# Scores of 21 of 32 attention units from split queries and keys in three passes, with a re-planned order, in a fused attention and two-layer kernel

## The chip, the cores and the metric

One core of a Trainium2 chip runs the whole program. The metric is the device time of one execution in microseconds (us). TensorE does the matrix products (PE in the rows, with its weight loads as PEld), VectorE (DVE), ScalarE (ACT) and GpSimd (POOL) the elementwise work, and SyncE (SP) issues most transfers.

## The reference

```python
scores = scale * np.matmul(q, k.transpose(0, 1, 3, 2))        # 4 batches, 8 heads, 576 rows, 64 deep
scores = np.where(causal, -1000000000.0, scores)
a = np.exp(scores - scores.max(-1, keepdims=True))
a /= a.sum(-1, keepdims=True) + 1e-09
local = np.matmul(a, v)
q_p = phi(q)                                                  # max(x + 1, exp(min(x, 0)))
mem_out = (q_p @ M_prev) / (q_p @ z_prev + 1e-6)
attn_out = g * mem_out + (1 - g) * local                      # g: a sigmoid per head
x = attn_out as 2304 tokens x 512
x = leaky_relu(x @ w_in) @ w_out                              # layer 1, 512 -> 2048 -> 512
x = (h - tanh(h)) @ w2_out, with h = x @ w2_in                # layer 2, the same shape
```

## The kernel before

**Two phases.** In the first, attention is done in 32 units (16 of kind B, then 16 of kind A), each for one batch and a pair of heads. A B unit has the query rows 256 to 575 against all keys, an A unit rows 0 to 255 against 256 keys. Mixed into this phase runs layer 1 for three blocks of 256 tokens. In the second phase layer 1 for the other blocks and then layer 2 run in a fixed loop of products 512 columns wide. Lines L910 and L988 are the layer products of the first phase, L1163 and L1200 those of the second.

**A unit's steps on TensorE**: scores (`score`, L647 for the tiles of 128 rows, L652 for the last 64 rows), the memory product (`mem`, L567), transposes of the memory part (L745) and of the probabilities (L779, L767), and the product with v (`pv`, L801). Scores are plain float32 products 64 deep: head 0 lies on partitions 0 to 63 and head 1 on 64 to 127, so the two heads of a pair use two halves of the array. The layer products are of type float32r, each number split beforehand into a high and a low part, in three products.

**The order** is written by a planner before the kernel is built. `Schedule.op` declares each piece of work with its expected duration on each engine that could do it; `Schedule.run` lets time go by, and each free engine takes the first piece in order of priority whose inputs are due and whose buffers (`RINGS`) are free. Attention goes ahead of layer work (`MOE_PE`), so layer products fill TensorE where attention isn't ready. The engines then execute that order strictly, however long things take. `SWITCH` is what the plan adds when TensorE goes from one kind of product to another (`mode`), `UNITS` the order of the units, `LEND` the number of first units that borrow the layer's PSUM buffers, `W1_FROM`, `W1_STEP`, `CUT` the priority of weight conversion on VectorE and ScalarE (L838 to L854), `CALM` how far ahead weight loads may queue.

**Between the phases** (`opened`, `load2`, `split_hi`, `split_lo`): when the last unit's output is copied and stored, two blocks are loaded back, `x2i`, one after the other through a single buffer; each is split into its high part (ScalarE) and its low part (VectorE), and the second phase's first product reads both blocks. The results of the third layer-1 block are copied out of PSUM (`g<-dn`) and stored (`x2s<-g`, L1008).

Of the kernel before, what the change touches and what calls it, by code (L numbers as in the profile page):

```python
# [9 lines left out]
F32 = mybir.dt.float32  # L10
# [22 lines left out]
RINGS = {  # L33
# [10 lines left out]

SWITCH = {(0, 1): 88.0, (2, 1): 88.0, (0, 2): 45.0}

CALM = 6000.0

# [18 lines left out]
def DVE(n):  # L67
    return 69 + 1.04 * n
# [202 lines left out]

OFFSET = {"load": 0, "memory": 0.3, "scores": -1, "values": 0.6}

MZ_APART = True

LEND = 6

LENT = ((0, 15), (1, 15), (1, 14))

UNITS = [(k, b, hp, hp % 2 if k == "A" or b < 1 else 0) for k in "BA" for b in range(4) for hp in range(4)]  # L280

# [3 lines left out]

AHEAD = 5

BIAS = {"act": 1.0, "dve": 1.5, "pool": 1.1}

W1_FROM, W1_STEP = (7.7, 15.7), 0.002  # L290

NARROW = 3

CUT = 2


@with_exitstack
def kernel(
# [14 lines left out]
    nc = tc.nc  # L313
# [159 lines left out]
    class Unit:  # L473
# [11 lines left out]
        def rows(self, t):  # L485
            return REST if t == 4 else 128

        def declare(self, pr, prev):
            kind, b, hp = self.kind, self.b, self.hp
# [13 lines left out]

            qk, v_ = new("qk"), new("v" if kind == "B" else "va")
            n0 = 0 if kind == "A" else NA
            qc, kc = (0, NA) if kind == "A" else (S, 0)

            def load_qk(e):
                qk.tile = att.tile([128, 896], F32, name="qk", bufs=RINGS["qk"])
# [82 lines left out]
            op([("dve", DVE(nqc))], phi_max, reads=[qk, ph], writes=[ph])  # L592
            order["p"] = op([("pe", nq * 195)], mem, reads=[ph, mz], alloc=[s, mo], after=in_order("p"))
            free_op([("dve", 75)], den_gate, reads=[s, gates], alloc=[dn], port=False)
            free_op([("dve", 110)], den_inv, reads=[dn], writes=[dn], port=False)
            free_op([("dve", DVE(nf))], mem_out, reads=[s, dn], writes=[mo], port=False)

            part_ = "scores"
# [6 lines left out]

            for tiles in ([[0, 1]] if kind == "A" else [[2], [3], [4]]):
                if not self.lend:
# [18 lines left out]
                def score(e, tiles=tiles, ss=ss):  # L626
# [6 lines left out]
                    for t in tiles:  # L633
                        nn, i, en = min(S, (t + 1) * 128), t - q0, et[t - q0].tag
                        if en[0] == "h":
                            m_, f_ = LENT[t - 2]
                            et[i].tile = wts.tile([128, 640] if t == 4 else [128, 2, nn], F32, name=f"w{m_}_{f_}")
                        else:
                            et[i].tile = att.tile([128, 640] if t == 4 else [128, 2, nn], F32, name=en, bufs=RINGS[en])
                        _, mx, c0 = made[t]  # L640
                        mx.tile = att.tile([128, 2], F32, name="mx", bufs=RINGS["mx"])
                        a, half = qc + i * 128, nn // 2
                        for k in range(1 if t < 4 else 2):
                            for j in range(2):
                                p = slice(64 * j, 64 * j + 64)
                                if t < 4:
                                    nc.tensor.matmul(  # L647
                                        ss[j].tile[:, c0:c0 + nn], lhsT=qk.tile[p, a:a + 128],
                                        rhs=qk.tile[p, kc:kc + nn], start=True, stop=True)
                                    continue  # L650
                                c = (j + k) % 2
                                nc.tensor.matmul(  # L652
                                    ss[c].tile[p, 0:half], lhsT=qk.tile[p, a:a + REST],
                                    rhs=qk.tile[p, kc + c * half:kc + (c + 1) * half], start=True, stop=True)

                order["s"] = op([("pe", {384: 847, 512: 1060, 576: 1117}[width])], score, reads=[qk], mode=1,
                                alloc=ss + [h for t in tiles for h in (et[t - q0], made[t][1])],
                                after=in_order("s") if tiles[0] == q0 else [order["s"]])
            for i in range(nq):
# [88 lines left out]

            op([("pe", nq * 109 - 60)], mem_tr, mode=2, reads=[mo], alloc=[o])
            pts, parts = {}, []  # L750
            for kt in range(nk):
# [35 lines left out]
                for j in range(len(ss)):  # L787
                    fresh = j == 0 and kt < 4
                    order["e"] = op(
                        [("pe", (nq - i0) * 109 * (3 - len(ss)) - 60)], lambda e, j=j, f=tr_e: f(e, j), mode=2,  # L790
                        reads=[et[i] for i in range(i0, nq)] + ([] if fresh else [pt]),
# [250 lines left out]
    for kind, b, hp, alt in UNITS:  # L1042
        u = Unit(kind, b, hp)
        u.alt, u.lend = alt, u_at < LEND
        u.declare((0, u_at), prev)
# [276 lines left out]
```

## Time and profile before

| | |
|---|---|
| median of 3 runs | 1019.87 us (1017.53 to 1020.28) |
| the profiled execution | 1019.15 us, of which the span of its instructions is 1017.4 |
| TensorE busy | 995.1 us of the span |
| VectorE, ScalarE, GpSimd busy | 702.8, 629.6, 196.9 us |
| first product of the second phase | 359.36 us after the start |

The profile page gives busy time per engine, the granted TensorE clock in slices, the chain of work that ended last and the costliest groups of instructions. Matmul durations in it overlap, since the engine is a pipeline: the pace of a stretch is read from the distance between starts.

### The profile page before, as it was taken

To read this page: it belongs to the slowest core of one execution; us is meant where nothing else is said; L and a number is where in the kernel's file an instruction comes from. 1 tells how busy PE (TensorE), PEld (TensorE's weight loads), DVE (VectorE), ACT (ScalarE), POOL (GpSimd) and SP (SyncE) were. 2 spreads that over 40 slices of the span, in tenths; PEclk is the share of its full clock that TensorE was granted. 3 is DMA by queue.
4 is the path that set the end of the run, shared out by engine and by line. 5 is a ranking of instruction groups with operands and counts; after the bars stand their busy time and mean duration, and the time that the engine had idled before them with its cause. 6 is when DMAs were issued, how large, how long until landed. Compare 5 with 4: busy or idle time off the path is not lost.

```text
span 1017.4 us, 16055 instructions
## 1 busy us (share of the span) xinstructions
PE 995.1 (98%) x5664; PEld 817.5 (80%) x5664; DVE 702.8 (69%) x1592; ACT 629.6 (62%) x1325; POOL 196.9 (19%) x174
## 2 busy tenths in 40 slices
PE   5899999999999999999999999999999999999998
PEld 3577877778888988888888888888888888888897
DVE  7999999555577366758650225877787787777775
ACT  6987787666598244334423436866676676676664
POOL 1100000000000022222224553222222222222221
PEclk9999999999999999999999999999999999999999
DMA  9564622212252156446534333100100100010010
GB/s 273 188 184 128 192 91 70 69 49 70 59 154 79 63 161 221 144 138 196 184 106 142 117 94 94 43 1 0 63 21 1 63 22 1 1 62 1 1 43 21
DMA packets 92993, 91.77 MB, mean 90 GB/s; under 512 B 45296, under 2 KB 72944, under 8 KB 92912
## 3 DMA queue, kind: packets, MB, share of 16 engines
q1 hardware_dynamic: 91696, 89.44, 28.5%
q10 hardware_dynamic: 1216, 1.31, 0.4%
q8 instruction: 44, 0.72, 0.3%
q14 instruction: 37, 0.30, 0.1%
HBM read 69.75 MB, written 20.97 MB: 89 GB/s over the span
## 4 chain that ended last, share of the span: by engine, by line
PE 91%; DVE 5%; DMA 2%; ACT 1%; issue 1%; SPq 0%; ACTq 0%
PE up L1163 32%; PE dn L1200 32%; PE up L910 6%; PE dn L988 6%; PE o L801 4%; PE s L779 4%; PE s L647 3%; DMA qk<-in_qkt_dram 2%; PE s L567 1%; PE o L745 1%; PE s L652 1%; DVE e L673 1%; DVE cv L849 1%; DVE w L673 1%; DVE e L729 0%
## 5 line engine op out<-in xcount | busy, mean ns | idle before, releaser
L1163 PE MATMUL up<-xs,w 128*128 128x512 f32 (+1 forms) x1536 | 346.1, 375 | 0.0
L1163 PEld LDWEIGHTS up<-xs,w 128*128 128x128 f32 x1536 | 275.8, 188 | 52.9
L468 POOL TENSOR_TENSOR gl<-gf,gh 128x512 fp32r<-128x512 f32 x119 | 154.9, 1301 | 591.7 <-ACT gh L1150 579.5
L1200 PE MATMUL dn<-w,gh 128*128 128x512 f32 x576 | 174.8, 389 | 0.0
L1140 DVE SCALAR_TENSOR_TENSOR gf<-u,w 128x512 f32<-128x512 f32 x72 | 83.8, 1165 | 67.7 <-ACT w L1137 67.6
L1200 PEld LDWEIGHTS dn<-w,gh 128*128 128x128 f32 x576 | 107.6, 188 | 22.0
L1200 PE MATMUL dn<-gh,w 128*128 128x512 f32 x384 | 118.3, 389 | 0.0
L1200 PE MATMUL dn<-w,gl 128*128 128x512 f32 x288 | 109.5, 389 | 0.0
L1117 ACT ACTIVATE gf<-up 128x512 f32<-128x512 f32 x48 | 28.6, 597 | 119.7 <-PE up L1163 116.4
L1131 ACT ACTIVATE u<-up 128x512 f32<-128x512 f32 x72 | 43.0, 598 | 91.8 <-PE up L1163 91.6
L693 ACT ACTIVATE e<-e,mx 128x256 f32<-128x256 f32 (+4 forms) x134 | 76.0, 569 | 21.8 <-DVE mx L673 13.6
L910 PE MATMUL up<-xs,w 128*128 128x256 f32 x576 | 86.8, 290 | 0.0
L1150 ACT ACTIVATE gh<-gf 128x512 fp32r<-128x512 f32 x120 | 74.6, 621 | 16.9 <-DVE gf L1143 16.8
L1200 PEld LDWEIGHTS dn<-gh,w 128*128 128x128 f32 x384 | 72.1, 188 | 15.0
L910 PEld LDWEIGHTS up<-xs,w 128*128 128x128 f32 x576 | 73.6, 189 | 4.7 <-issue 4.7
L1200 PE MATMUL dn<-gl,w 128*128 128x512 f32 x192 | 74.7, 389 | 0.0
L1200 PEld LDWEIGHTS dn<-w,gl 128*128 128x128 f32 x288 | 54.0, 188 | 11.3
L455 ACT ACTIVATE pt<-s 128x320 f32<-128x320 f32 (+4 forms) x132 | 52.7, 440 | 15.9 <-PE s L779 9.3
L673 DVE CUSTOM_DVE_ANT_0 e<-s,mask 128x128 f32<-128x128 f32 (+4 forms) x114 | 46.8, 455 | 22.3 <-PE s L647 19.3
L779 PE MATMUL s<-identr,e 128*128 128x128 f32 x404 | 56.9, 279 | 4.4 <-ACT e L727 1.8
L1143 DVE COPY_PREDICATED gf<-mk,up 128x512 f32<-128x512 int32 x72 | 53.7, 746 | 7.4
L988 PE MATMUL dn<-gh,w 128*128 128x256 f32 x384 | 54.7, 286 | 0.4 <-ACT gh L455 0.4
(130 smaller groups left out, 1506.2 us busy)
## 6 DMA issues: line engine op xcount, KB each, us to landing
w<-in_moe_w_out_dram SPq DMA_DIRECT2D x16, 512.0 KB, 5.5
w<-vs SPq DMA_DIRECT2D x32, 256.0 KB, 2.6
qk<-in_qkt_dram SPq DMA_DIRECT2D x16, 448.0 KB, 3.6
w<-in_moe_w_in_dram SPq DMA_DIRECT2D x14, 512.0 KB, 5.8
v<-in_v_dram SPq DMA_DIRECT2D x16, 320.0 KB, 3.1
x2i<-x2s SPq DMA_DIRECT2D x9, 512.0 KB, 4.1
qk<-in_qkt_dram SPq DMA_DIRECT2D x16, 256.0 KB, 2.8
u<-in_moe_w_in_dram SPq DMA_DIRECT2D x16, 256.0 KB, 2.9
```

The source lines that it names most:

```text
L455: nc.scalar.activation(out=out, in_=in_, func=AF.Copy)
L468: (nc.vector if e == "dve" else nc.gpsimd).tensor_tensor(out=out, in0=in_, in1=high, op=ALU.subtract)
L673: nc.vector.tensor_tensor_reduce(out=out, in0=in0, in1=in1, scale=-scale, scalar=mx.tile[:, 0:1] if t == 4 and j else BIG, op0=ALU.add, op ...
L693: nc.scalar.activation(out=x, in_=x, func=AF.Exp, scale=-1.0, bias=mx.tile[:, k:k + 1], accum_out=sm.tile[:, 2 * i + j:2 * i + j + 1])
L779: nc.tensor.transpose(ss[j].tile[:, a:a + 128], x, ident)
L910: nc.tensor.matmul(ps()[:, s, :], lhsT=w[:, wh * 512 + kt * 128:wh * 512 + (kt + 1) * 128], rhs=xs()[:, xh, kt, :], start=(kt == 0 and j = ...
L988: nc.tensor.matmul(dn[m // 2].tile[:, m % 2, :], lhsT=w[:, wh * 512 + m * 128:wh * 512 + (m + 1) * 128], rhs=gg.tile[:, s * 256:(s + 1) * ...
L1140: nc.vector.scalar_tensor_tensor(out=g, in0=u, scalar=lin, in1=w, op0=ALU.mult, op1=ALU.add)
L1143: nc.vector.copy_predicated(out=g, mask=mk.bitcast(I32), data=h)
L1150: nc.scalar.activation(out=gh, in_=g, func=AF.Copy)
L1163: nc.tensor.matmul(ps[:, s * n:(s + 1) * n], lhsT=w[:, wh * 512 + kt * 128:wh * 512 + (kt + 1) * 128], rhs=xs[:, xh, kt, 0:n], start=(kt = ...
L1200: nc.tensor.matmul(dn, lhsT=lhs, rhs=rhs, start=(fs[0] == 0 and s == 0 and j == 0), stop=(f == NF - 1 and j == 2))
```

## The change

In the units from the 12th on (`SPLIT`: 5 of kind B, 16 of kind A) the queries and keys are copied into a high part `qh` and a low part `ql` of type float32r, and the scores of the tiles of 128 rows come from three products (high by high, high by low, low by high) that add up in PSUM. The tile of the last 64 rows of a B unit stays float32, and is now the first of its unit. `qk`, `qh` and `ql` have one buffer each; the first 11 units use the three in turn as raw buffers. `mz` and `va` go from two buffers to one. The plan counts the new products with its own durations (`PASSED`) and as the same kind as the layer products (mode 0), `mem` as a kind of its own, and has new values for switches, priorities and the order of the units. The loop of the second phase is the same.

```diff
 RINGS = {
-    "qk": 2, "xr": 1, "mz": 2, "v": 1, "va": 2, "ph": 1, "dnm": 2, "mo": 1, "mx": 6, "sm": 3,
+    "qk": 1, "qh": 1, "ql": 1, "xr": 1, "mz": 1, "v": 1, "va": 1, "ph": 1, "dnm": 2, "mo": 1, "mx": 6, "sm": 3,
...
-SWITCH = {(0, 1): 88.0, (2, 1): 88.0, (0, 2): 45.0}
-
-CALM = 6000.0
+SWITCH = {
+    (0, 1): 90.0, (2, 1): 92.0, (2, 0): -81.0, (0, 2): 4.0, (0, 3): 90.0, (2, 3): 55.0, (3, 1): 160.0,
+    (3, 2): 90.0, (1, 3): 10.0,
+}
+
+CALM = 2000.0
...
-LEND = 6
+LEND = 7
+
+PASSED = {384: 528, 512: 696}
+
+SPLIT = 11
...
-W1_FROM, W1_STEP = (7.7, 15.7), 0.002
+W1_FROM, W1_STEP = (27.2, 10.8), 0.2
...
-CUT = 2
+CUT = 6
...
+            if self.split:
+                qh, ql = new("qh"), new("ql")
+
+                def q_hi(e):
+                    qh.tile = att.tile([128, 896], F32R, name="qh", bufs=RINGS["qh"])
+                    copy(e, qh.tile[:, 0:n], qk.tile[:, 0:n])
+
+                def q_lo(e):
+                    ql.tile = att.tile([128, 896], F32R, name="ql", bufs=RINGS["ql"])
+                    low(e, ql.tile[:, 0:n], qk.tile[:, 0:n], qh.tile.bitcast(F32)[:, 0:n])
...
-            for tiles in ([[0, 1]] if kind == "A" else [[2], [3], [4]]):
+            for tiles in ([[0, 1]] if kind == "A" else [[4], [2], [3]] if self.split else [[2], [3], [4]]):
...
+                        passes = [(qk.tile, qk.tile)]
+                        if self.passed(t):
+                            passes = [(qh.tile, qh.tile), (qh.tile, ql.tile), (ql.tile, qh.tile)]
                         for k in range(1 if t < 4 else 2):
...
+                            for n_, (x, y) in enumerate(passes):
+                                flags = dict(start=n_ == 0, stop=n_ == len(passes) - 1)
+                                for j in range(2):
+                                    p = slice(64 * j, 64 * j + 64)
+                                    if t < 4:
+                                        nc.tensor.matmul(
+                                            ss[j].tile[:, c0:c0 + nn], lhsT=x[p, a:a + 128],
+                                            rhs=y[p, kc:kc + nn], **flags)
+                                        continue
...
-                order["s"] = op([("pe", {384: 847, 512: 1060, 576: 1117}[width])], score, reads=[qk], mode=1,
+                order["s"] = op(
+                    [("pe", PASSED[width] if self.passed(tiles[0]) else {384: 847, 512: 1060, 576: 1117}[width])], score,
+                    reads=[qh, ql] if self.passed(tiles[0]) else [qk], mode=0 if self.passed(tiles[0]) else 1,
```

On TensorE, at the scores of an A unit (the last whose scores stand in the order; a row is one line of the program with its output, its moving and its stationary operand, and the output's shape), before there were:

```order
L801 MATMUL o<-pt,va 64x256 x2
L801 MATMUL o<-pt,va 64x128 x2
L647 MATMUL s<-qk 128x128 x2
L647 MATMUL s<-qk 128x256 x2
L745 MATMUL o<-identr,mo 128x128 x2
```

and now:

```order
L948 MATMUL up<-xs,w_13_2081 128x256 x3
L683 MATMUL s<-qh 128x128 x2
L683 MATMUL s<-ql,qh 128x128 x2
L683 MATMUL s<-qh,ql 128x128 x2
L683 MATMUL s<-qh 128x256 x2
L683 MATMUL s<-ql,qh 128x256 x2
L683 MATMUL s<-qh,ql 128x256 x2
L783 MATMUL o<-identr,mo 128x128 x2
```

Four products became twelve, two heads at a time; here they now stand after layer products (`up`) and not after another product of the attention.

On ScalarE, at the start of the program (`ph` is the memory's query map, `e` and `w_15` the exponentials of units 0 and 1, `ginv` the gate, whose values come by a transfer, `cv` the first step of weight conversion), before:

```order
L552 ACTIVATE ph<-qk 128x320
L556 ACTIVATE ph<-ph 128x320
L693 ACTIVATE e_186,sm<-e_186,mx 128x384 x2
L838 ACTIVATE cv<-w_0_65 128x512
L693 ACTIVATE e_196,sm<-e_196,mx 128x512 x2
L693 ACTIVATE e_213,sm<-e_213,mx 128x576
L1018 ACTIVATE ginv<-ginv 128x8
```

and now:

```order
L569 ACTIVATE ph<-qk 128x320
L573 ACTIVATE ph<-ph 128x320
L1056 ACTIVATE ginv<-ginv 128x8
L731 ACTIVATE e_184,sm<-e_184,mx 128x384 x2
L876 ACTIVATE cv<-w_0_65 128x512
L876 ACTIVATE cv<-w_1_66 128x512
L731 ACTIVATE e_194,sm<-e_194,mx 128x512 x2
L731 ACTIVATE e_222,sm<-e_222,mx 128x576
```

The gate's exponential moved ahead of the first unit's exponentials. On VectorE the rest of the gate moved with it, to behind the first two row maxima.

At the end of the first phase, on TensorE from the last product with v on, before (after these rows come the rest of this group of 24 `dn`, seven more groups of 24, the last two both `dn`, and then the second phase):

```order
L801 MATMUL o<-pt,va 64x256 x2
L801 MATMUL o<-pt,va 64x128 x2
L910 MATMUL up<-xs,w_8_1494 128x256 x9
L910 MATMUL up<-xs,w_9_1561 128x256 x12
L988 MATMUL dn_3965<-gh,w_6_1377 128x256 x2
```

and now (after these rows come the other 46 `dn` products, and then the second phase):

```order
L839 MATMUL o<-pt,va 64x256 x2
L839 MATMUL o<-pt,va 64x128 x2
L948 MATMUL up<-xs,w_15_2296 128x256 x9
L1026 MATMUL dn_3894<-gh,w_12_2188 128x256 x2
```

Behind the last product of the attention stood 21 + 24 x 8 = 213 layer products, and now stand 9 + 48 = 57. In the same place SyncE's queue (x1s is the store of the last block, x2i the loads of two blocks) held before:

```order
L924 DMA x1s_141<-x 128x1024
L1080 DMA x2i<-x1s_137 128x1024
L1080 DMA x2i<-x1s_138 128x1024
L1008 DMA x2s_130<-g 128x512 x2
L386 DMA u<-in_moe_w_in_dram 128x2x256
```

and now:

```order
L962 DMA x1s_141<-x 128x1024
L1119 DMA x2i<-x1s_137 128x1024
L1046 DMA x2s_130<-g 128x512 x2
L1119 DMA x2i<-x1s_138 128x1024
L400 DMA u<-in_moe_w_in_dram 128x2x256
```

The second load moved behind the two stores of the third block's results.

## Rows read from the trace of the kernel before

**Rows 1.** The page: the span, and each engine's busy time in it.

```profile
span 1017.4 us, 16055 instructions
PE 995.1 (98%) x5664; PEld 817.5 (80%) x5664; DVE 702.8 (69%) x1592; ACT 629.6 (62%) x1325; POOL 196.9 (19%) x174
```

**Rows 2.** Three stretches: start:end length, busy time by engine, clock, DMA share, GB/s.

```profile
9.13:22.78 13.65, 7.21 (x42) 3.69 (x38) 13.20 (x56) 11.33 (x28) 1.35 (x2) 1.00 0.98 295
22.78:26.20 3.42, 3.27 (x15) 2.94 (x17) 3.42 (x9) 1.99 (x6) 0.00 (x0) 0.50 1.05 380
...
250.00:300.00 50.00, 50.00 (x432) 43.23 (x430) 33.56 (x150) 36.89 (x118) 0.00 (x0) 1.00 0.34 93
```

**Rows 3.** Two steps of weight conversion on VectorE: busy us, mean ns.

```profile
L849 DVE SCALAR_TENSOR_TENSOR cv<-w,cv 128x512 int32<-128x512 int32 x32 | 21.7, 681 | 0.0
...
L844 DVE TENSOR_SCALAR cv<-cv 128x512 int32<-128x512 int32 x32 | 13.1, 416 | 0.0
```

**Rows 4.** The timeline on TensorE at two score steps: start, length, what.

```profile
251.31 0.93 PE L647 MATMUL s<-qk 64*128 64x128 f32 x8
252.17 0.87 PE L801 MATMUL o<-pt,va 128*64 128x256 f32 x8
...
100.22 1.13 PE L647 MATMUL s<-qk 64*128 64x512 f32 x4
101.28 0.55 PE L745 MATMUL o<-identr,mo 128*128 128x128 f32 x3
```

**Rows 5.** Weight loads and the first layer product after scores; then its mean.

```profile
100.21 0.30 PEld L647 LDWEIGHTS s<-qk 64*128 64x128 f32 x4
100.32 0.19 PEld L647 LDWEIGHTS s<-qk 64*128 64x128 f32 x2
...
96.77 0.38 PE L988 MATMUL dn<-gh,w 128*128 128x256 f32 x1
...
L988 PE MATMUL dn<-gh,w 128*128 128x256 f32 x384 | 54.7, 286 | 0.4 <-ACT gh L455 0.4
```

**Rows 6.** The timeline on TensorE around one visit to score products.

```profile
84.97 0.72 PE L988 MATMUL dn<-gh,w 128*128 128x256 f32 x4
85.61 1.19 PE L652 MATMUL s<-qk 64*64 64x288 f32 x8
86.73 1.68 PE L988 MATMUL dn<-gh,w 128*128 128x256 f32 x12
```

**Rows 7.** The gate's transfer: issue, time to landing; ScalarE's first exponential.

```profile
6.45 1.66 SPq L1015 DMA_DIRECT2D ginv<-in_beta_dram  x1
...
DMA to landing us min/median/max: 4.4/4.4/4.4
...
7.40 0.61 ACT L693 ACTIVATE e<-e,mx 128x384 f32<-128x384 f32 x1 [1.33 <-DVE mx L673]
```

**Rows 8.** The timeline between the phases, and the copies of the third block.

```profile
334.24 2.72 PE L910 MATMUL up<-xs,w 128*128 128x256 f32 x21
335.20 7.88 SPq L1080 DMA_DIRECT2D x2i<-x1s  x2
340.42 1.06 ACT L455 ACTIVATE xs<-x2i 128x1024 fp32r<-128x1024 f32 x1 [2.82 <-DMA x2i<-x1s]
342.76 0.32 SPq L1080 DMA_DIRECT2D x2i<-x1s  x1
346.08 1.06 ACT L455 ACTIVATE xs<-x2i 128x1024 fp32r<-128x1024 f32 x1 [2.89 <-DMA x2i<-x1s]
347.18 1.23 DVE L1094 TENSOR_TENSOR xs<-x2i,xs 128x1024 fp32r<-128x1024 f32 x1 [2.73 <-ACT xs L455]
359.20 3.16 PE L1163 MATMUL up<-xs,w 128*128 128x512 f32 x13
...
L455 ACT ACTIVATE g<-dn 128x512 f32<-128x512 f32 x6 | 3.4, 597 | 5.2 <-PE dn L988 5.2
```

More of the change, by code (lines that the diff above doesn't have):

```diff
@@ L270 @@
 MOE_PE = 1
-OFFSET = {"load": 0, "memory": 0.3, "scores": -1, "values": 0.6}
+OFFSET = {'load': -0.2, 'memory': 0.4, 'scores': -0.8, 'values': 0.7}
 MZ_APART = True
-LEND = 6
+LEND = 7
+PASSED = {384: 528, 512: 696}
+SPLIT = 11
 LENT = ((0, 15), (1, 15), (1, 14))
-UNITS = [(k, b, hp, hp % 2 if k == "A" or b < 1 else 0) for k in "BA" for b in range(4) for hp in range(4)]
+UNITS = [
[6 rows of a table added]
+]
 GROUPS = {"A": ((0, 2),), "B": ((0, 1), (1, 2), (2, 3))}
 EARLY = 2
-AHEAD = 5
-BIAS = {"act": 1.0, "dve": 1.5, "pool": 1.1}
-W1_FROM, W1_STEP = (7.7, 15.7), 0.002
+AHEAD = 4
+BIAS = {'act': 1.0, 'dve': 1.7, 'pool': 1.1}
+W1_FROM, W1_STEP = (27.2, 10.8), 0.2
 NARROW = 3
-CUT = 2
+CUT = 6
 @with_exitstack
@@ L486, in rows, with passed @@
             return REST if t == 4 else 128
+        def passed(self, t):
+            return self.split and t < 4
         def declare(self, pr, prev):
@@ L501, in in_order @@
                 return [prev.order[name]] if prev else []
-            qk, v_ = new("qk"), new("v" if kind == "B" else "va")
+            qk, v_ = new(self.raw), new("v" if kind == "B" else "va")
             n0 = 0 if kind == "A" else NA
@@ L592, in declare @@
             op([("dve", DVE(nqc))], phi_max, reads=[qk, ph], writes=[ph])
-            order["p"] = op([("pe", nq * 195)], mem, reads=[ph, mz], alloc=[s, mo], after=in_order("p"))
+            order["p"] = op([("pe", nq * 195)], mem, mode=3, reads=[ph, mz], alloc=[s, mo], after=in_order("p"))
             free_op([("dve", 75)], den_gate, reads=[s, gates], alloc=[dn], port=False)
@@ L656, in declare @@
-                order["s"] = op([("pe", {384: 847, 512: 1060, 576: 1117}[width])], score, reads=[qk], mode=1,
+                            for n_, (x, y) in enumerate(passes):
[7 more added lines that the diff above has]
+                                        continue
+                                    c = (j + k) % 2
+                                    nc.tensor.matmul(
+                                        ss[c].tile[p, 0:half], lhsT=x[p, a:a + REST],
+                                        rhs=y[p, kc + c * half:kc + (c + 1) * half], **flags)
@@ L657, in declare @@
+                order["s"] = op(
+                    [("pe", PASSED[width] if self.passed(tiles[0]) else {384: 847, 512: 1060, 576: 1117}[width])], score,
+                    reads=[qh, ql] if self.passed(tiles[0]) else [qk], mode=0 if self.passed(tiles[0]) else 1,
                                 alloc=ss + [h for t in tiles for h in (et[t - q0], made[t][1])],
-                                after=in_order("s") if tiles[0] == q0 else [order["s"]])
+                    after=in_order("s") if "s" not in order else [order["s"]])
@@ L789, in declare @@
                     order["e"] = op(
-                        [("pe", (nq - i0) * 109 * (3 - len(ss)) - 60)], lambda e, j=j, f=tr_e: f(e, j), mode=2,
+                        [("pe", 109 if kt == 4 else (nq - i0) * 109 * (3 - len(ss)))], lambda e, j=j, f=tr_e: f(e, j), mode=2,
                         reads=[et[i] for i in range(i0, nq)] + ([] if fresh else [pt]),
@@ L1043 @@
         u = Unit(kind, b, hp)
-        u.alt, u.lend = alt, u_at < LEND
+        u.alt, u.lend, u.split = alt, u_at < LEND, u_at >= SPLIT
+        u.raw = "qk" if u.split else ("qk", "qh", "ql")[u_at % 3]
         u.declare((0, u_at), prev)
```

16 lines of the change are left out of this document (4 added, 12 removed), and 6 rows, old and new, of the table UNITS.

## The prediction

> **What bounds the kernel now.** The page comes first: TensorE is busy for 98% of the span [rows 1], so time can come only from fewer TensorE cycles, from the few stretches where it waits, or from new waits. The second phase is the same in both kernels, so only the moment at which it starts counts. The table of stretches shows where TensorE waits now: between 9.13 and 22.78 us it is busy for 7.21 us of 13.65 while VectorE is busy for 13.20, and in the next 3.42 us the granted clock is half (1.2 GHz instead of 2.4) [rows 2]. So the start hangs on VectorE. Later it turns round: from 250 to 300 us TensorE is busy throughout, VectorE for 33.6 us of 50 and ScalarE for 36.9 [rows 2]. The timeline between the phases shows the last thing to read: after the last attention product (done by 334.24) TensorE has layer products until 359.20, 25 us without a gap, while two loads and two splits go by on the side until 348.4 (347.18 + 1.23) [rows 8]. That cover is what the change touches.
>
> **Score products.** For an A unit the float32 scores take 251.31 to 252.17, that is 0.86 us [rows 4]. A layer product of 256 columns goes at 0.117 us (213 of them from 334.24 to 359.20 [rows 8]). Two heads run side by side; at four passes 128 + 256 columns should stream in 4 x 384/256 x 0.107 = 0.64 us (0.107 is 256 columns at 2.4 GHz), and the 512 columns of a B tile in 0.85 us, of the 1.06 from 100.22 to 101.28 [rows 4]. The remaining 0.2 us does not depend on the columns. Three float32r passes would stream 0.48 and 0.64 us, if nothing else sets the pace.
>
> Something does: each product loads its own weights. The first two pairs of loads of a score step start at 100.21 and 100.32 [rows 5], 0.11 us apart, and the streaming hides only later ones. Float32r loads are no shorter: the first layer product after scores, whose load nothing hides, takes 0.38 us where the mean is 0.286 [rows 5], so the load is about 0.1 us. A pass over 128 columns streams in 0.053 us but cannot go faster than its load, and one over 256 columns takes the load's time anyway, so an A unit has six pair steps of at least 0.107 to 0.11 us: 0.64 to 0.66 us, the same as in float32. **The 16 A units gain nothing.** In the 5 B units the tiles of 384 and 512 columns (streams of 0.64 and 0.85 us) become 0.48 and 0.64, a gain of 0.37 us a unit, 1.9 us together. Against that, 256 columns go at 0.117 and not at 0.107 us; 0.01 us for each longer step adds up to 0.8 us at most, and I take half of it.
>
> The Trainium skill's page "FP8 and Floating Point Precision" (section "TensorE Precision Notes") says that true FP32 takes four passes through the array. Going by passes alone, three would save a quarter of every unit's stream, 0.16 us more in each A unit; the sum would then be 2.6 us lower. The rows show the load as the floor there, and no row has a float32r product below 256 columns, so the load decides in my sum.
>
> **Visits.** Going from 128-row products to the half-array products costs time in itself. Around one visit, 4 layer products take 84.97 to 85.61, 0.64 us instead of 0.47, and the score step 85.61 to 86.73, 1.12 instead of the 0.96 that 4 x 2 x 288 columns stream [rows 6]: 0.33 us a visit. The split passes use the same half-array shape, so they pay it as well, though the plan counts them as layer products. In the order the visits from other shapes rise from 60 to 65, and steps with another such step right before them fall from 31 to 24; at 0.33 and half of it, + 0.5 us. Score products and visits together: - 1.9 + 0.4 + 0.5 = **- 1 us** (from - 3.6 without the load's floor to + 0.5).
>
> **The splitting itself.** 21 copies and 21 subtractions go to engines that have 13 to 16 us of every 50 free [rows 2]; some 1.3 us per 6 us unit fits, and I cost it at nothing. The single buffers of `qk`, `qh`, `ql`, `va` and `mz` make loads start later; they are covered as long as the order holds layer products in front of the waiting step. I take 0, and 3 us as the upper end (seven reloads of `mz`, under half a microsecond each).
>
> **The start.** Two things, both on VectorE. Ahead of the last row sum of the sixth unit the order has 31 steps of weight conversion, where 39 stood, one subtraction less and three copies less, but two scalings more. Eight steps at 0.42 to 0.68 us [rows 3] are 4.4 us, the rest some 2 us net; since successive steps overlap a little, 5.3 us of VectorE time. The other way goes the gate. Its transfer is issued at 6.45 us and lands 4.4 us later, at 10.9 [rows 7]. Now its exponential is ahead of the first unit's on ScalarE, which began at 7.40 [rows 7], and VectorE has the rest of the gate after two row maxima, at some 8 us. Both engines stand until about 11.1: 3.2 us lost where VectorE is the limit. Behind them wait the other row maxima, whose PSUM buffers the second unit's scores need, and so TensorE. Net **- 2 us** (from - 8, all of the idle time there and the clock's dip, to + 2).
>
> **Between the phases.** After the last attention product the order now has 57 layer products, 6.7 us, where 213 stood. The chain of loads is no shorter. Counted from that product's end (334.24 [rows 8]), the first load is issued at + 0.96, its copy starts at + 6.2 and ends at + 7.2, and the subtraction frees the buffer at + 8.5 (the second load's issue at 342.76). But the second load now also stands in SyncE's queue behind the two stores of the third block. Their copies (0.6 us each [rows 8]) can start on ScalarE only when the last layer product is done (+ 7.0) and the first split's copy too (+ 7.2): done at + 8.5. Two issues of some 0.3 us put the second load at + 8.9. Landing takes 3.3 us as now (342.76 to 346.08), up to 5.2 with stores on the way as for the first load (335.20 to 340.42) [rows 8]; copy and subtraction, 346.08 to 348.41, another 2.3: ready between + 14.5 and + 16.4. TensorE stands from + 6.8 on: 7.7 to 9.6 us, I take **+ 8.5**. A wait like those of the start also costs the clock: the stretch at half clock lasted 3.42 us [rows 2], so half of that is lost again: **+ 1.7** (0 to 2).
>
> **The sum.** - 1 - 2 + 8.5 + 1.7 = + 7.2 us on the profiled execution's 1019.15: 1026. (That execution is 0.7 us below the median of the three runs; I don't correct for it.)
>
> **The rivals.**
> Faster: the plan's prices are right. Then an A unit's scores take 0.53 us and a B unit's two tiles 0.53 and 0.70 with no visit, instead of 0.86 + 0.17 and of about 2.0: 16 x 0.5 + 5 x 0.78 = 11.9 us less, 11.4 with the 0.5 from the other visits. The end stays: - 11.4 - 2 + 8.5 + 1.7 = - 3.2, or 1016. It decides as soon as the passes save more than about 8 us together. For it speaks that nothing in the trace shows split passes on half the array; against it the load's 0.11 us and the visit in rows 5 and 6. The page "TensorEngine Tiling (Array Packing)" of the Trainium skill (section "Key Properties") says that a change of tiling mode drains TensorE; by that rule the visits stay and this rival falls, and the rows agree with their 0.33 us.
> Slower still: the narrow pass isn't quick. No row has one; at float32's pace of 0.21 us per 128 columns an A unit costs 0.32 us more, 16 of them 5.1 us: 1031. Two heads that don't run side by side would be worse yet.
> About the same: VectorE's lighter start gives back nearly all the waiting there, - 8 instead of - 2: 1020.
>
> **How the numbers follow.** My forecast has 0.57, the plan's prices 0.20, the narrow pass 0.11, the large gain at the start 0.12. The likeliest one's own range is 1021 to 1031 (the end's 7.7 to 9.6, the clock's 0 to 2, the start's and the buffers' ends). Leaving out the outer half of the plan's case and of the slow pass gives 1015 to 1032. A change below 0.3%, 3 us, is about what this measurement can't tell from none. Faster by more: half of the plan's case and a little of the others, 0.15; within: the rest of that case, the large gain, the low end of mine, 0.26; slower: 0.59.
>
> **What would show it.** Right, if after the last `o<-pt,va` product TensorE has 57 layer products and then a gap of 8 to 9 us that ends with the second split's subtraction, with the clock halved after it; if six pairs of an A unit's scores are 0.11 us apart and the step takes 0.8 us or more; if ScalarE's first exponential of a score starts near 11 us and not at 7.4. Wrong, if an A unit's scores take 0.55 us, if the layer products after scores start without a delay, or if TensorE's idle time before 70 us falls by more than 5 us.

## The result, and the profile after

The changed kernel takes 1029.08 us (median of 4 runs, 1028.70 to 1029.38); the kernel before took 1019.31 beside it. The ratio is 1.0098, with a 95% interval of 1.0080 to 1.0115: slower by one per cent. The profiled execution took 1028.94 us, 9.8 more than that of the kernel before.

The page of the changed kernel, its span and busy times, answers to [rows 1]:

```profile
span 1027.2 us, 16265 instructions
...
PE 998.9 (97%) x5748; PEld 824.9 (80%) x5748; DVE 707.9 (69%) x1593; ACT 639.0 (62%) x1350; POOL 211.0 (21%) x189
```

The span grew by 9.8 us and TensorE's busy time by 3.8, so 6 us of it are new waiting. The longest wait in the list of TensorE's waits (total, times, longest) shows where:

```profile
PE up L1202 <- ACT xs L469: 7.9, 1, 7.9
```

L1202 is the first product of the second phase. Before the change that product started at 359.20 us [rows 8] (the table ahead of the prediction has 359.36); now it starts at 366.69. The timeline between the phases answers to [rows 8]; the last attention product is done when the row of 351.85 begins:

```profile
351.85 1.32 PE L948 MATMUL up<-xs,w 128*128 128x256 f32 x9
...
352.76 0.43 SPq L1119 DMA_DIRECT2D x2i<-x1s  x1
...
357.68 1.09 PE L1026 MATMUL dn<-gl,w 128*128 128x256 f32 x8
358.15 1.06 ACT L469 ACTIVATE xs<-x2i 128x1024 fp32r<-128x1024 f32 x1 [3.68 <-DMA x2i<-x1s]
...
359.25 1.23 DVE L1133 TENSOR_TENSOR xs<-x2i,xs 128x1024 fp32r<-128x1024 f32 x1 [4.05 <-ACT xs L469]
359.72 0.81 SPq L1046 DMA_DIRECT2D x2s<-g  x2
360.63 0.41 SPq L1119 DMA_DIRECT2D x2i<-x1s  x1
...
365.58 1.06 ACT L469 ACTIVATE xs<-x2i 128x1024 fp32r<-128x1024 f32 x1 [5.40 <-DMA x2i<-x1s]
...
366.69 0.80 PE L1202 MATMUL up<-xs,w 128*128 128x512 f32 x1 [7.92 <-ACT xs L469]
367.95 7.24 PE L1202 MATMUL up<-xs,w 128*128 128x512 f32 x25 [0.46 <-DVE xs L1133]
```

The 57 layer products behind the last attention product end near 358.8. The second load, issued at 360.63, is copied only from 365.58 on, and TensorE stands for 7.92 + 0.46 = 8.4 us, with one product between the two waits. Windows over the two stretches at half clock and over the time up to the end of the last attention product, of the changed kernel; then that time for the kernel before:

```profile
0.00:351.85 351.85, 336.14 (x2716) 272.31 (x2716) 273.06 (x930) 263.58 (x690) 29.84 (x54) 0.99 0.40 116
12.34:19.17 6.83, 4.46 (x11) 2.19 (x11) 6.41 (x30) 6.41 (x17) 1.38 (x3) 0.50 0.73 278
363.91:370.74 6.83, 3.58 (x8) 2.50 (x9) 1.23 (x1) 1.06 (x1) 0.00 (x0) 0.50 0.45 152
```

```profile
0.00:334.24 334.24, 316.28 (x2476) 247.76 (x2476) 265.96 (x922) 251.49 (x663) 15.71 (x39) 0.99 0.42 122
```

The last attention product ends 17.6 us later than before, but 156 layer products (213 - 57) that used to follow it now stand ahead of it, 18.3 us at the 0.117 us that each took there. Up to there the change breaks about even; the loss is made between the phases. TensorE's 3.58 us at half clock behind the gap cost another 1.8.

The score steps answer to [rows 4]: an A unit, then the two split tiles of a B unit.

```profile
334.87 0.33 PE L683 MATMUL s<-qh 64*128 64x128 f32 x2
335.04 0.27 PE L683 MATMUL s<-ql,qh 64*128 64x128 f32 x2
335.15 0.28 PE L683 MATMUL s<-qh,ql 64*128 64x128 f32 x2
335.26 0.33 PE L683 MATMUL s<-qh 64*128 64x256 f32 x2
335.43 0.28 PE L683 MATMUL s<-ql,qh 64*128 64x256 f32 x2
335.55 0.28 PE L683 MATMUL s<-qh,ql 64*128 64x256 f32 x2
335.75 0.50 PE L1026 MATMUL dn<-gh,w 128*128 128x256 f32 x2
```

```profile
213.36 0.45 PE L683 MATMUL s<-qh 64*128 64x384 f32 x2
...
214.09 0.62 PE L948 MATMUL up<-xs,w 128*128 128x256 f32 x3
...
215.33 0.50 PE L683 MATMUL s<-qh 64*128 64x512 f32 x2
...
216.22 0.98 PE L948 MATMUL up<-xs,w 128*128 128x256 f32 x6
```

The A step takes 334.87 to 335.75, 0.88 us, 0.02 to 0.03 more than in float32 [rows 4]. In each of its two tiles the first pair of products takes 0.17 us until the next pair starts; the others follow at 0.11 (128 columns) and 0.12 (256 columns). All other A units but one, which has a wait in it, take 0.88 or 0.89 as well, against 0.86 in each of the 16 before. The weight loads of the same step, on their own queue, stand 0.11 apart from the first to the last:

```profile
334.87 0.19 PEld L683 LDWEIGHTS s<-qh 64*128 64x128 f32 x2
334.98 0.19 PEld L683 LDWEIGHTS s<-ql,qh 64*128 64x128 f32 x2
...
335.43 0.19 PEld L683 LDWEIGHTS s<-qh,ql 64*128 64x128 f32 x2
```

The B tiles take 0.73 and 0.89 us. In float32 the 512 columns took 1.06 [rows 4], and the 384 took 0.85, in the timeline of the kernel before:

```profile
95.92 0.92 PE L647 MATMUL s<-qk 64*128 64x384 f32 x4
96.77 0.50 PE L988 MATMUL dn<-gh,w 128*128 128x256 f32 x2
```

At the start ScalarE stands until the gate has landed, and VectorE and TensorE behind it, where ScalarE's first exponential began at 7.40 before [rows 7]; from the timelines of the three engines:

```profile
11.12 0.21 ACT L1056 ACTIVATE ginv<-ginv 128x8 f32<-128x8 f32 x1 [5.36 <-DMA ginv<-in_beta_dram]
11.23 0.60 ACT L731 ACTIVATE e<-e,mx 128x384 f32<-128x384 f32 x1
...
11.36 0.17 DVE L1059 TENSOR_SCALAR ginv<-ginv 128x8 f32<-128x8 f32 x1 [3.82 <-ACT ginv L1056]
...
14.71 1.67 PE L683 MATMUL up<-qh 64*128 64x384 f32 x3 [4.17 <-DVE mx L711]
```

### The profile page after: what moved, and what is told of

Read it like the earlier page. It is cut to its first block, busy times and chain, and to the rows that moved or that the text cites. A ratio compares the mean times of both kernels' runs of the same rounds, so it can differ in the third digit from the quotient of the medians.

```text
span 1027.2 us, 16265 instructions
## 1 busy us (share of the span) xinstructions
PE 998.9 (97%) x5748; PEld 824.9 (80%) x5748; DVE 707.9 (69%) x1593; ACT 639.0 (62%) x1350; POOL 211.0 (21%) x189
## 4 chain that ended last, share of the span: by engine, by line
PE 88%; DVE 6%; DMA 4%; ACT 1%; issue 1%; SPq 0%; POOL 0%; POOLq 0%; ACTq 0%
PE up L1202 32%; PE dn L1239 32%; PE up L948 6%; PE dn L1026 5%; PE s L817 3%; PE o L839 3%; PE s L683 3%; DMA qk<-in_qkt_dram 1%; PE s L584 1%; DVE e L711 1%; PE s L688 1%; DMA x2i<-x1s 1%; PE o L783 1%; DVE cv L887 1%; DMA ginv<-in_beta_dram 0%
## 5 line engine op out<-in xcount | busy, mean ns | idle before, releaser
L1202 PE MATMUL up<-xs,w 128*128 128x512 f32 (+1 forms) x1536 | 348.0, 377 | 8.4 <-ACT xs L469 7.9
L1202 PEld LDWEIGHTS up<-xs,w 128*128 128x128 f32 x1536 | 276.7, 188 | 62.3 <-ACT xs L469 8.1
L469 ACT ACTIVATE pt<-s 128x320 f32<-128x320 f32 (+4 forms) x146 | 57.2, 441 | 19.0 <-PE s L817 16.1
L711 DVE CUSTOM_DVE_ANT_0 e<-s,mask 128x128 f32<-128x128 f32 (+4 forms) x109 | 44.2, 450 | 21.7 <-PE s L683 12.5
L1026 PE MATMUL dn<-gh,w 128*128 128x256 f32 x384 | 58.6, 290 | 0.0
```

The source lines that it names most:

```text
L469: nc.scalar.activation(out=out, in_=in_, func=AF.Copy)
L711: nc.vector.tensor_tensor_reduce(out=out, in0=in0, in1=in1, scale=-scale, scalar=mx.tile[:, 0:1] if t == 4 and j else BIG, op0=ALU.add, op ...
L1026: nc.tensor.matmul(dn[m // 2].tile[:, m % 2, :], lhsT=w[:, wh * 512 + m * 128:wh * 512 + (m + 1) * 128], rhs=gg.tile[:, s * 256:(s + 1) * ...
L1202: nc.tensor.matmul(ps[:, s * n:(s + 1) * n], lhsT=w[:, wh * 512 + kt * 128:wh * 512 + (kt + 1) * 128], rhs=xs[:, xh, kt, 0:n], start=(kt = ...
```

## The experiments

The theory that went into the runs: the loss is the gap and its clock, and the gap opens because the split A units, with one buffer each for the raw and the split operands, make the planner spend layer products between their steps that are missing as cover at the end. The rivals: the passes themselves are slow; the plan's wrong prices draw the products forward; the new order loses the time whatever the scores are.

**Is it the passes?** The A units keep every copy, subtraction, buffer and place in the order; only the products differ, and no longer read the low part.

```diff
-                            passes = [(qh.tile, qh.tile), (qh.tile, ql.tile), (ql.tile, qh.tile)]
+                            passes = [(qh.tile, qh.tile)] + [(qh.tile, ql.tile), (ql.tile, qh.tile)] * (kind == "B")
...
+                                if kind == "A":
+                                    x, y = x.bitcast(F32), y.bitcast(F32)
```

> The changed kernel with all its copies, subtractions, buffers, waits and its whole order, but an A unit's scores are one float32 product of the high part with itself instead of three passes, so the low parts are left out of them; the B units keep their passes. Theory 1 (the split's loop costs, not the passes): TensorE's A score steps get shorter by only 0.03 us each, and the time is the change's within 1 us, 1027.5 to 1029.5, with the gap at the end of the first phase still 8 us. Rival, the three passes are what costs (through TensorE's mode, clock or drains): 1022 or less.

Measured: 1029.34 us, ratio to before 1.0089 (1.0076 to 1.0101), with TensorE's wait at the second phase as good as unchanged:

```profile
PE up L1204 <- ACT xs L469: 7.4, 1, 7.4
```

So the three passes of the A units cost nothing against float32 and gain nothing, as far as the medians can tell (to some 2 us; the rows above make it 16 x 0.03); what surrounds them costs.

**All passes out, A passes out.** Two kernels, each planned anew with the change's other numbers: one in which no unit is split, and one in which only the five B units are. Unsplit units take their operands in the three buffers in turn.

```diff
-SPLIT = 11
+SPLIT = 40
```

> All 32 units take float32 scores; queries and keys go through the three buffers in turn, and the order is planned anew with the change's other numbers. In the order 195 layer products stand after the last attention product (57 in the change, 213 before), some 22.8 us at 0.117, more than the 16 us that the two loads and splits take. Theory 1, the loss is the gap between the phases, because the split units' single buffers let the plan use up the layer products: no gap, no half clock behind it, so -8.4 - 2, and undoing the passes costs +1.0 (5 B units +1.47, 16 A units -0.45) and three more visits +1: about 1020.7, range 1019 to 1022. Rival 2, the passes themselves cost much more than their rows show: below 1017. Rival 3, the new order, switch costs and single buffers lose the time whatever the scores are: 1027 or more.

```diff
-        u.alt, u.lend, u.split = alt, u_at < LEND, u_at >= SPLIT
+        u.alt, u.lend, u.split = alt, u_at < LEND, SPLIT <= u_at < 16
```

> One part alone: only the five B units (12th to 16th) are split, the 16 A units take float32 scores and their queries and keys rotate through the three buffers; prices and all other numbers are the change's. In the order 192 layer products stand after the last attention product, with 63 visits. Theory 1 (it is the A units' split that uses up the cover, and they gain nothing by the passes): no gap, -10.4, the A units' passes undone -0.45, visits -1: about 1017.2, range 1016 to 1019. Rival, the A units' passes do gain (0.16 us each by the number of passes): 1019.5 or more, 2.6 us above that.

Measured: without any split 1023.95 us, ratio 1.0043 (1.0030 to 1.0056); with the B units alone 1018.93, 0.9989 (0.9980 to 0.9998). Both have no gap between the phases. The B version gives back the 10 us. The other is 3 us above what I expected and above the range of 1019 to 1022: its order has waits of its own, 3.7 us of idle TensorE in this window (the B version idles 0.7 there) and 1.3 between 250 and 300 us:

```profile
150.00:200.00 50.00, 46.34 (x349) 36.59 (x348) 34.83 (x106) 35.82 (x83) 2.45 (x5) 0.97 0.25 75
```

A new plan alone is thus worth some microseconds either way, and a comparison of two plans tells a mechanism only where the windows show it.

**Do wrong prices draw the products forward?**

```diff
-PASSED = {384: 528, 512: 696}
+PASSED = {("A", 384): 875, ("B", 384): 716, ("B", 512): 897}
...
-                    [("pe", PASSED[width] if self.passed(tiles[0]) else {384: 847, 512: 1060, 576: 1117}[width])], score,
-                    reads=[qh, ql] if self.passed(tiles[0]) else [qk], mode=0 if self.passed(tiles[0]) else 1,
+                    [("pe", PASSED[kind, width] if self.passed(tiles[0]) else {384: 847, 512: 1060, 576: 1117}[width])], score,
+                    reads=[qh, ql] if self.passed(tiles[0]) else [qk], mode=1,
```

> The passes stay; the plan is told what they measured (A 0.875, B 0.716 and 0.897 us instead of 0.528, 0.528 and 0.696) and that they are half-array products (mode 1). In the order 69 layer products then stand after the last attention product, and there are 62 visits instead of 66. Theory 1 (the single buffers use up the layer products, not the prices): 12 products more make the gap 1.4 us shorter, four visits less -1.3: about 1026.5, range 1025 to 1028, with a gap of some 7 us and the half clock still there. Rival, the wrong prices are what pulled the products ahead: the gap goes and the time is 1020 or less.

Measured: 1026.30 us, 1.0065 (1.0052 to 1.0078). The gap is there, 4.4 us of it (3.9 until the copy) and not the 7 that I had expected, with the stretch at half clock behind it; 1.4 us of waiting came up between 300 and 340 us instead. (The profiled execution took 1028.45, 2 us above the median; up to 160 us, where the two orders are still the same, it is 2.3 us behind the change's.) The prices are a part of the loss, some 3 us with the visits, not its cause.

**Can the products simply be held back?**

```diff
-                    alloc=[ps] if one else [], prio=(MOE_PE, 2 * seq), order=one)
+                    alloc=[ps] if one else [], prio=(MOE_PE, 2 * seq), order=one,
+                    after=[ends[31]] if n == NARROW - 1 and p >= NP - 4 and one else ())
```

> The changed kernel, but the last four pairs of the third block's layer products may start only behind the last unit's scores and stores: 192 layer products stand after the last attention product. Passes, prices and buffers are the change's. Theory 1 (the gap and its clock are the loss, 8.4 + 2): no gap, and TensorE finds other work before, so about 1018.7, range 1017.5 to 1021. Rival, the products are missed where they stood: TensorE waits in the attention part instead, between 250 and 335 us, for the same 8 to 10 us: 1027 to 1030, with the idle time in the windows before the last attention product.

Measured: 1032.12 us, 1.0120 (1.0107 to 1.0133), slower than the change. The rival held. The gap at the end is gone. TensorE waits in the attention instead, for 5.9 us of 40, and behind that the clock falls (a mean of 0.74 from 340 to 360):

```profile
300.00:340.00 40.00, 34.08 (x302) 27.53 (x299) 31.99 (x136) 29.85 (x100) 0.00 (x0) 1.00 0.39 103
340.00:360.00 20.00, 18.29 (x121) 15.13 (x120) 5.64 (x19) 7.96 (x20) 0.00 (x0) 0.74 0.26 86
```

So my theory was half of it. The products were not spent carelessly: the split units need them. Only all four pairs were held, 192 products where the loads and splits need some 140 (16 us at 0.117); whether holding fewer would pay was not tried. I looked at the units' own waiting instead.

**What makes the units need them?** In the changed kernel's timeline (SyncE's queue and VectorE's steps on `qk`) the next load of `qk` is issued once the feature map `ph`, its last reader, is done:

```profile
310.15 0.34 SPq L527 DMA_DIRECT2D qk<-in_qkt_dram  x1
313.57 0.42 DVE L471 CAST qh<-qk 128x512 fp32r<-128x512 f32 x1
314.02 0.69 DVE L482 TENSOR_TENSOR ql<-qk,qh 128x512 fp32r<-128x512 f32 x1
314.88 0.43 DVE L576 SCALAR_TENSOR_TENSOR ph<-qk,ph 128x256 f32<-128x256 f32 x1
316.06 0.42 SPq L527 DMA_DIRECT2D qk<-in_qkt_dram  x1
```

5.9 us lie between these two loads (8.1 and 6.2 between the next ones). The load lands after 2.5 us, and VectorE, which is on other work, copies it 0.9 us later. With a second buffer the next load can go ahead of the unit's copy, subtraction and feature map:

```diff
...
-        u.raw = "qk" if u.split else ("qk", "qh", "ql")[u_at % 3]
+        u.raw = ("qk", "qh", "ql")[u_at % 3] if not u.split else ("qk", "e4")[u_at % 2] if kind == "A" else "qk"
```

> The changed kernel, but the 16 A units load their queries and keys into two buffers in turn (qk and e4, which no A unit uses otherwise) instead of one. Passes, splitting and prices are the change's. In the order 94 layer products then stand after the last attention product (57 in the change) and there are 62 visits instead of 66. Theory 1 (with one raw buffer each A unit runs a loop of load, copy, subtraction and feature map of about 5.4 us before the next load, while TensorE has some 3 us of work for it, so the layer products are used up as filling): the last attention product ends earlier, the gap is shorter by 37 x 0.117 = 4.3 us, and the visits give -1.3: about 1023.5, range 1021.5 to 1025. Rival, the loop is not what paces the units (the passes or the other engines' extra work are): 1027 or more, with the average A unit still at 6 us or more.

Measured: 1019.27 us, 0.9998 (0.9989 to 1.0007): the whole loss is gone, with all passes in place. That is below the 1021.5 to 1025 that I expected. The waits at the second phase, and its loads and splits, in this kernel:

```profile
PE up L1202 <- DVE xs L1133: 0.8, 1, 0.8
PE up L1202 <- ACT xs L469: 0.7, 1, 0.7
```

```profile
345.87 1.90 PE L1026 MATMUL dn<-gh,w 128*128 128x256 f32 x14
...
346.88 6.80 SPq L1119 DMA_DIRECT2D x2i<-x1s  x2
351.02 1.06 ACT L469 ACTIVATE xs<-x2i 128x1024 fp32r<-128x1024 f32 x1 [4.54 <-DMA x2i<-x1s]
...
356.68 1.06 ACT L469 ACTIVATE xs<-x2i 128x1024 fp32r<-128x1024 f32 x1 [3.46 <-DMA x2i<-x1s]
```

The gap is 1.5 us instead of 8.4. The 37 more products give 4.3 of that. The rest is that the chain got shorter: counted from the end of the last attention product the second copy starts at + 10.8 (356.68 - 345.87), in the change at + 13.7 (365.58 - 351.85). Both loads landed sooner, after 4.0 and 3.3 us against 5.3 and 4.9. During the second one (issued at 353.37 in this run, ahead of the third block's stores again) the DMA engines were busy for less than half of the time; in the change, where stores and weight loads are issued around it, all the time. First this run, then the change:

```profile
353.37:356.68 3.31, 3.31 (x30) 3.31 (x30) 0.58 (x1) 0.00 (x0) 0.00 (x0) 1.00 0.47 158
```

```profile
360.63:365.58 4.95, 0.00 (x0) 0.00 (x0) 0.00 (x0) 0.00 (x0) 0.00 (x0) 0.83 1.02 314
```

Which of these transfers delays it is not shown. The shorter chain (2.6) and the half clock that went with the gap (1.8) make up the 4 us by which it came out below 1023.5.

Is it the buffer, or just another new order? The two profiled executions differ by 10.1 us. The gap gives 6.9 of them and the clock behind it 1.8. Up to 240 us the order is the same in both, and there this execution is already 0.9 us ahead, which no edit made. The 37 products cost some 0.6 us less behind the attention than in it (the price is worked out below). That is 10.2 together, so nothing is left for the rest of the order. The A units did not become much quicker: from the first to the last of their products with v it takes 96.8 us, 6.45 a unit, where the change takes 101.0, 6.73. An average of 6 us or more had been named as a sign of the rival; the time, far below the rival's 1027, speaks against it.

The Trainium skill's page "Trainium Kernel Development and Optimization" (section "Best Practices") advises double-buffering so that transfers lie beside computing. This run agrees with it by 9.8 us.

**One buffer without the split.** The version with only the B units split, but the A units' operands in one buffer:

```diff
-        u.alt, u.lend, u.split = alt, u_at < LEND, u_at >= SPLIT
-        u.raw = "qk" if u.split else ("qk", "qh", "ql")[u_at % 3]
+        u.alt, u.lend, u.split = alt, u_at < LEND, SPLIT <= u_at < 16
+        u.raw = "qk" if u.split or kind == "A" else ("qk", "qh", "ql")[u_at % 3]
```

> As the run with only the B units split (1018.9), but the A units, unsplit, load their queries and keys into one buffer (qk) instead of three in turn: the single raw buffer without the split. In the order 102 layer products stand after the last attention product (192 there, 57 in the change). Theory 1 (the single buffer is the larger part of what uses up the layer products, and what counts is how many are left against the 13 to 16 us of loads and splits): 102 x 0.117 = 11.9 us of cover, a gap of 1.5 to 4 us, a half-clock stretch behind it or not: 1020.5 to 1024. Rival, the split alone uses them up, or a single buffer costs nothing because it is covered: 1019 or less. Second rival, the single buffer alone does all the harm: 1027 or more.

Measured: 1021.11 us, 1.0014 (1.0004 to 1.0024), with a gap of 0.8 us (expected 1.5 to 4). So the single buffer alone takes 90 of the 192 products of the version with only the B units split and costs 2 us: 0.8 for the gap, and an estimated 1.4 because 90 products now stand among the attention steps (priced below). The split takes another 45, down to 57, and these are the dear ones, since with them the cover falls below what the loads and splits last. Counted the other way round, the split takes 98 with two raw buffers (94 are left) and the step to one buffer 37 more. So neither is the cause by itself: the gap needs both the split and the single buffer. What in the split takes them even with two raw buffers is open: the single `qh` and `ql`, or the time of copy and subtraction on the engines.

**The start.** The plan is told that the gate lands 2 us later, on top of the version with only the B units split; then with right prices as well.

```diff
-                            o.lat = self.landed - mine
+                            o.lat = self.landed - mine + (2000.0 if o.dma == (4096,) else 0.0)
...
```

> As the run with only the B units split, but the plan is told that the gate's transfer lands 2 us later, so that ScalarE takes the first unit's exponentials and VectorE the other row maxima of that unit ahead of the gate. Theory (the gate costs VectorE and TensorE about 3.5 us in a stretch where VectorE is the limit): ScalarE's first exponential of a score near 7.4 instead of 11.2 us, VectorE's wait of 3.8 us gone, and of it 2 to 3.5 us reach the end: 1015.5 to 1017.5 against 1018.9. Rival, the time is given back before 70 us because something else holds the start (the second unit's loads): 1018.5 or more.

> As the run before, and the plan is told the measured times of the passes in the B units and that they are half-array products. 198 layer products after the last attention product, 59 visits instead of 60: within 1 us of the run before, 1015 to 1017.5; a version that is to beat the kernel before. Rival: the order that comes out has new waits, 1019 or more.

Measured: 1024.31 us, 1.0046 (1.0032 to 1.0061), 7 us above what I expected, and 1019.42, 1.0001 (0.9988 to 1.0014), 2 us above. Of the first version the profiled execution took 1022.23; its eleven runs spread from 1021.0 to 1028.4, more than those of any other. ScalarE's first exponential did move to 6.95 us. TensorE's busy time by stretch, first with the late gate, then in the version with only the B units split without it:

```profile
0.00:27.00 27.00, 19.08 (x110) 10.58 (x111) 20.70 (x88) 20.58 (x51) 6.72 (x19) 1.00 0.84 256
27.00:70.00 43.00, 37.73 (x281) 25.19 (x281) 42.26 (x133) 37.61 (x99) 6.38 (x10) 1.00 0.63 181
```

```profile
0.00:27.00 27.00, 17.27 (x75) 9.15 (x77) 16.52 (x69) 15.74 (x38) 4.80 (x16) 0.87 0.74 222
27.00:70.00 43.00, 40.63 (x302) 26.27 (x298) 42.82 (x148) 39.15 (x103) 5.27 (x9) 1.00 0.60 173
```

TensorE gains 1.8 us before 27 and no clock is lost there, but it loses 2.9 from there to 70 and 2.8 between 150 and 200 (busy for 46.56 us of 50 against 49.32), where the gate has no part. I take these for the new order again, and for the spread of the runs I have no cause. What the gate's wait is worth at the end stays open.

**Towards a better version.** Two buffers with right prices; two buffers for the values too; only the B units split, with right prices.

```diff
-            qk, v_ = new(self.raw), new("v" if kind == "B" else "va")
+            qk, v_ = new(self.raw), new("v" if kind == "B" else ("va", "v")[hp % 2])
...
```

> As the run with two raw buffers (1019.3), and the plan is told the measured times of the passes and that they are half-array products. In the order 124 layer products stand after the last attention product (94 there) and 59 visits (62 there). Theory 1: the remaining gap of 1.5 us goes, three visits less give -1: about 1017, range 1015.5 to 1018.5. Rival, with the gap gone the prices of the plan no longer matter: 1018.8 or more.

> As the run with two raw buffers, and the A units' values are also loaded into two buffers in turn (va and v, which no A unit uses otherwise); prices are the change's. 128 layer products after the last attention product, 59 visits. Theory 1 (what lengthens an A unit's loop is its single buffers, the values' among them): the gap goes and the visits give -1: about 1017, range 1015.5 to 1018.5. Rival, the values' buffer was covered: 1018.8 or more.

> As the run with only the B units split (1018.9), and the plan is told the measured times of the passes and that they are half-array products: 150 layer products after the last attention product, some 17.5 us against the 16 that the loads and splits take, and 60 visits instead of 63. About 1018, range 1016.5 to 1019; if the gap comes back, 1020.

Measured: 1018.10 us, 0.9985 (0.9974 to 0.9996); 1017.57, 0.9978 (0.9968 to 0.9988); and 1017.00, 0.9966 (0.9953 to 0.9978). The last has the lowest median of the study: 12 us under the change, and a third of a per cent under the kernel before. Its interval overlaps with those of the other two, so their order among themselves is not settled. In it the A units keep float32 scores. The other two came out within what was expected of them; that the values' second buffer adds something to the raw one's is likely, but the two also differ in their whole order.

## Why the prediction came out as it did

The forecast of 1026 and the sign were right, 3 us too low. By its own terms, in us:

| term | predicted | measured |
|---|---|---|
| A units' passes | 0 | +0.5 (16 x 0.03) |
| B units' passes | -1.9 + 0.4 | -1.5 (5 x (0.12 + 0.17)) |
| visits | +0.5 | some -0.7, a remainder |
| layer products that moved forward | not in the sum | +2.7 (21.0 - 18.3) |
| start and other waits | -2 | -2.3, and +0.6 of clock |
| gap between the phases | +8.5 | +8.4 |
| half clock behind it | +1.7 | +1.8 |
| sum | +7.2 | +9.5, of 9.8 |

**Passes: right.** The loads stand 0.11 us apart, and so do the 128-column passes but for each tile's first; an A unit gains nothing, as the prediction read from [rows 5] and the run without the A passes confirmed. The Trainium skill's page "FP8 and Floating Point Precision" (section "TensorE Precision Notes") counts four passes for float32, by which three would save a quarter. The B tile of 512 columns saved 16%, the A step nothing: at these widths the count of passes did not decide, and the measurement does.

**The layer products that moved forward: left out, and most of the miss.** TensorE is busy for 336.14 - 316.28 = 19.9 us more up to the last attention product. Counted from each product's start to the next start on TensorE, without the waits (over all products this adds up to the same 316.28 and 336.14), the 939 layer products ahead of it took 124.56 us before, and the 1095 now take 145.56: 21.0 us more. That is 0.133 us for each in both kernels, where those behind the last attention product go at 0.117. So a layer product among attention steps costs 0.016 us more, before the change as after it, and 156 of them have moved there. The prediction priced the 57 that are left behind, and put nothing for the others' new place.

**Visits: no sign of the + 0.5.** Without these 21.0, the clock (0.6: half of 4.46 less half of the 3.27 in [rows 2]) and the passes (-1.0), -0.7 is left of the 19.9 for the visits and all other work. No run isolates it.

**Start: right in size, by luck as much as by reading.** TensorE's idle time up to the last attention product fell from 18.0 to 15.7 us; up to 70 us it fell by 2.7, under the 5 that would have shown the forecast wrong. What was foretold of it is in the rows: the exponential at 11.23, VectorE's 3.82 us of idle time, TensorE waiting for a row maximum. But the start differs as much between executions. Nine of the experiments have the change's order on TensorE up to 160 us at least, and the same product there (the 201st) starts between 43.1 and 45.8 us in them, at 44.1 in the change. In the run without the A passes the half clock at the start lasts half as long as the 6.83 us in the change:

```profile
14.17:17.58 3.41, 3.39 (x8) 1.70 (x8) 3.08 (x16) 3.16 (x9) 0.81 (x2) 0.50 0.71 286
```

So one pair of executions settles a term of 2 us neither way, and the two parts of it, VectorE's lighter work and the gate, were not measured apart.

**Between the phases: right,** in the order foretold, except that most of the wait ends with the copy (`ACT xs`) and only the last 0.46 us with the subtraction. That gap and clock agree to 0.1 us is in part luck. The 8.5 was the middle of 7.7 to 9.6. The second load's place behind the stores cost next to nothing: the subtraction freed the buffer at 360.48 (359.25 + 1.23), the stores were issued by 360.53, and the load went at 360.63. It landed after 4.9 us, near the upper of the two times allowed for, 3.3 and 5.2. And the clock stayed at half for 6.83 us and not for 3.42, but TensorE stood for the better part of the first 4 of them.

**Buffers: right as a cost, missed as a cause.** I took 0 for the single buffers, "covered as long as the order holds layer products in front of the waiting step". That is what happened, and the cover was paid with the products that were lacking at the end. The two terms were one: giving back one buffer took all but 1.5 us of the gap. A reader of the prediction would have looked for the cure at the end of the phase, where the one run with products held back found none.

**The plan's prices right: fell.** The steps take 0.88, 0.73 and 0.89 us and not 0.53, 0.53 and 0.70. **Narrow pass slow: fell,** at 0.11 us a pair. **VectorE's lighter start:** TensorE's idle time fell by 2.3 us and not by 8.

## What to carry to other kernels

Where independent work fills every wait, a longer chain in one part shows up as missing cover somewhere else: count how much filling each stage uses before and after (here 156 products, found behind the last attention product), and look for the cause where it is used. Price the filling at what it costs in its new place, here 0.133 and not 0.117 us each. Buffers given up to pay for a feature cost what their waiting steps need as filling, not what the trace shows as idle. A split into narrower passes paid here at 384 and 512 columns, where a pass streams longer than its weights load, and not at 128 and 256. Before a difference between two profiles is given to an edit, compare the stretch that the edit left alone: here it differed by up to 2.7 us.

## What the runs showed of the hardware

A float32r product on half the array goes at 0.11 us a pair for 128 columns and, between two others (335.43 to 335.55), at 0.12 for 256: from 128 to 256 columns its width costs next to nothing. The second load of `x2i` landed 3.3 us after its issue where the DMA engines were busy for 0.46 of the time (342.76 to 346.08 before the change) and 0.47 (353.37 to 356.68 with two raw buffers), and 4.9 us after it where they were busy throughout (360.63 to 365.58 in the change). The first load, of the same size, doesn't follow that share: it took 5.1, 4.0 and 5.3 us at 0.56, 0.71 and 0.57. With one and the same order at the start, TensorE's clock was at half there for 3.41 us in one execution and for 6.83 in another.
